# Eighty unread 384-column products behind the rounded exponentials of the first ten units

## The chip, the core and the metric

The program runs on one core of a Trainium2 chip. A core has a matrix engine (TensorE, PE in the profile, with its weight loads shown as PEld), VectorE (DVE), ScalarE (ACT), GpSimd (POOL), SyncE (SP, which here only issues transfers) and 16 DMA engines. Each engine works through its own list of instructions in order and waits on semaphores of the others. The metric is the device time of one execution in microseconds (us); a comparison takes the median of several runs.

## The reference

Biased attention is followed by a two-layer network with a sigmoid gate. Shapes: 4 batches, 8 heads, 576 positions, head size 64; 2304 tokens of width 512, hidden width 2048.

```python
scores = q @ k.T / 8
x = log1p(|i - j|) / log1p(max(i, 1))
bias = relu(x * w1 + b1) @ w2              # 32 hidden values, one result per head
attn = softmax(scores + bias); out = attn @ v
x = out as [2304, 512]
h = x @ w_in; g = h * sigmoid(1.702 * h); result = g @ w_out
```

Everything comes and goes as 4-byte floats, the weights as 8-byte floats that the kernel takes apart as 32-bit words.

## The kernel before

**Precision.** Each large product is made of three products of 16-bit halves: an operand is scaled, rounded to 16 bits (the high part), and the rest is kept as a second 16-bit tile (the low part, made by `lo_part`, L218, or at L382, L420, L508).

**Units.** The attention is cut into 72 units: two heads of one batch for one chunk of 128 query rows (a chunk has 64 rows at the end). The first 36 units are for batches 0 and 1. For unit u the written program does, in this order:

- `emit_s`: 12 products into the score tile `sp` (L349). The pool `ps_s` has one such tile, so the scores of the next unit wait until this one is read.
- `emit_soft1`: per head VectorE adds the bias tile `bt` and finds the maximum (L365, called *the maximum* here), ScalarE takes the exponential (L369), VectorE makes the reciprocal of the sum (L376, L377), ScalarE or VectorE writes the rounded exponentials into `hl` (L381 or L379, called *the rounding*), VectorE writes their low part (L382). Then one DMA transposes `hl` into `aT` (L391, issued by SP).
- `emit_av`, two to four units later: 30 products of `aT` with the values (L414) into a tile `ot`, which VectorE reads out to `xT` (L419, L420).
- steps of the network on token blocks that are finished: `emit_m1` (12 products into `hp`, L492, then L498, L500, L505 or L507, L508) and `emit_m2` (products into `op`, L522).
- a share of splitting the weights (`split_w`): three bit operations (L456, L459, L462), a rounding (L468) and a low part (L218) for each of 32 pieces: one piece after each of the units 0 to 7, four after each of the units 8 to 13.
- a share of the bias tables (`bias_hidden`, four activations L163 or L165; `bias_products`, 16 products L183 and L185; the copy L189; the store L190), up to unit 28.
- loads and transposes for later units, among them `trans_k_own` (L285, L292, with read-outs L287, L294 and L218), which makes the keys `kT` of heads 4 to 7: of batch 0 after unit 2 (needed by unit 4), of batch 1 after unit 4 (needed by unit 6).

**Banks.** The pool `ps_h` has two banks, which are given out in turn, in the written order, to `pc`, `kt`, `kp`, some `qp`, every `ot` and every `hp`. Whoever gets a bank waits until its last user has been read or, where nobody reads it, written.

**Order.** The order on each engine isn't the written one: a scheduler goes through the program with its own estimate of time and lets an instruction go ahead as soon as its operands and banks are free by that estimate. One instruction more can so move others far away.

Of the kernel before, what the change touches and what calls it, by code (L numbers as in the profile page):

```python
# [7 lines left out]
F32 = mybir.dt.float32  # L8
# [12 lines left out]
def kernel(  # L21
# [26 lines left out]
    nc = tc.nc  # L48
# [41 lines left out]
    ps_h = ctx.enter_context(tc.tile_pool(name="ps_h", bufs=2, space=PSUM))  # L90
# [120 lines left out]
    def stage(shape, dt, tag, name):  # L211
        return wk.tile(shape, dt, tag=tag, name=name, bufs=BUFS[tag])
# [143 lines left out]
    def emit_soft1(u):  # L356
        bt = bt_t[u]
        at = wk.tile([128, 2 * S], F32, tag="a32", name="a32", bufs=BUFS["a32"])
        mx = wk.tile([128, 2], F32, tag="mx", name="mx")
        sm = wk.tile([128, 2], F32, tag="sm", name="sm", bufs=6)  # L360
        hl = wk.tile([128, 2, 2 * S], F16, tag="hl", name="hl", bufs=BUFS["hl"])
        for a in range(2):
            cs = slice(S * a, S * a + S)

            nc.vector.tensor_tensor_reduce(  # L365
                out=at[:, cs], in0=s_ps.pop((u, a))[:, 0:S], in1=bt[:, cs], scale=-1.0 / BS, scalar=3.0e38,
                op0=ALU.add, op1=ALU.min, accum_out=mx[:, a:a + 1],
            )
            nc.scalar.activation(  # L369
                out=at[:, cs], in_=at[:, cs], func=ACTF.Exp, scale=-1.0, bias=mx[:, a:a + 1],  # L370
                accum_out=sm[:, a:a + 1],
            )
        for a in range(2):
            cs = slice(S * a, S * a + S)
            r = sm[:, a:a + 1]
            nc.vector.tensor_scalar(out=r, in0=r, scalar1=1.0e-9, scalar2=1.0 / AS, op0=ALU.add, op1=ALU.mult)  # L376
            nc.vector.reciprocal(out=r, in_=r)  # L377
            if a < VEC_EXP.get(u, 0):
                nc.vector.tensor_scalar(out=hl[:, 0, cs], in0=at[:, cs], scalar1=r, scalar2=None, op0=ALU.mult)  # L379
            else:  # L380
                nc.scalar.activation(out=hl[:, 0, cs], in_=at[:, cs], func=ACTF.Identity, scale=r)  # L381
            nc.vector.scalar_tensor_tensor(  # L382
                out=hl[:, 1, cs], in0=at[:, cs], scalar=r, in1=hl[:, 0, cs], op0=ALU.mult, op1=ALU.subtract
            )

        if u in AT_W:
            x = 8 * 2 * DM + 18 * 128 * AT_W[u]
            t = wo16.rearrange("p f x d -> p (f x d)")[:, x:x + 18 * 128].rearrange("p (c n) -> p c n", c=18)
        else:
            t = stage([128, 18, 128], F16, "aT" if u <= max(BIAS_A) or u % 4 < 2 else "ht", "aT")  # L390
        nc.sync.dma_start_transpose(out=t, in_=hl.rearrange("p x n -> p (x n)"))  # L391
        aT[u] = t
# [262 lines left out]
    for u in range(NU + 2):  # L655
        if u < NU:
            emit_s(u)
            emit_soft1(u)
        ready = NF * sum(1 for x in last_unit if x < av)
        late = u - AV_LAG.get(u, 2) in last_unit[1:]  # L660
        if not late:
            msteps(ready, STEPS_A.get(u, 1))
        while av <= u - AV_LAG.get(u, 2):
            emit_av(av)
            av += 1
        if late:
            msteps(ready, STEPS_A.get(u, 1))
        elif u - 2 == last_unit[0]:
            ready = NF
        if u < len(W_STEPS):  # L670
            weights_to(w_done[1] + W_STEPS[u])
        if u in BIAS_A:
            bias_first()
        msteps(ready, STEPS_B.get(u, 1))
        bias_second()
        if u in BIAS_B:
            bias_first()
            bias_second()
        if u + BIAS_AHEAD < NU:
            bias_get(u + BIAS_AHEAD)  # L680
        for fn, args in todo.get(u, ()):
            fn(*args)
# [56 lines left out]
```

## Time and profile before

| | us |
|---|---|
| median of 3 runs | 725.68 (724.52 to 728.96) |
| the profiled execution | 725.27 |
| its span, first to last instruction | 723.5 |
| TensorE busy | 642.0 (89%) |
| VectorE busy | 514.7 (71%) |
| ScalarE busy | 408.1 (56%) |
| mean granted clock of TensorE | 0.959 of full |

A busy share is a mean over the whole span. The kernel has a front part, in which the bias tables, the splitting of the weights and the first units go on together, and a long rest, in which TensorE is nearly always busy, so the engines have to be read by stretches. The granted clock has two levels, 1.2 and 2.4 GHz; a mean of 0.75 means half of the time at either.

### The profile page before, as it was taken

The numbers are of one execution on the slowest core, as the hardware profiler recorded it, in microseconds if no ns is written. First come the engines' busy times: TensorE is split into PE (matmuls) and PEld (weight loads), VectorE is DVE, ScalarE is ACT, GpSimd is POOL, SyncE is SP. The second block draws the span as 40 slices with busy tenths as digits, with TensorE's granted clock in tenths as the row PEclk, the third lists the DMA queues.
The fourth block names the chain that finished last, engine by engine and source line by source line (L and its number), as shares of the span: only waits on it lengthen the run. The fifth ranks groups of instructions, "written<-read, shape, count | busy, mean of one in ns | idle before, by whom it ended". The sixth has DMA issues, their size and how long they took to land. (4 is left out here: it accounts for less than half of the span.)

```text
span 723.5 us, 17516 instructions
## 1 busy us (share of the span) xinstructions
PE 642.0 (89%) x6888; PEld 385.0 (53%) x6888; DVE 514.7 (71%) x1416; ACT 408.1 (56%) x847; POOL 133.9 (19%) x194
## 2 busy tenths in 40 slices
PE   5655777869969999999979899899999999999997
PEld 3212333425536655656646465566666666666765
DVE  6865998798957766777677877855775896775321
ACT  6897978686558655665544446743443453343133
POOL 1202000111201111212221112121222222212222
PEclk9967978998989999999999999999999999999999
DMA  9889999968997656867576789955564475745000
GB/s 241 236 259 237 240 241 289 259 158 221 216 175 174 132 116 134 178 149 154 127 173 115 164 146 148 189 134 107 100 129 106 100 167 126 122 77 96 2 31 15
DMA packets 230771, 111.80 MB, mean 155 GB/s; under 512 B 210720, under 2 KB 214944, under 8 KB 230688
## 3 DMA queue, kind: packets, MB, share of 16 engines
q1 hardware_dynamic: 222592, 94.65, 62.7%
q10 hardware_dynamic: 7952, 15.43, 7.0%
q8 instruction: 54, 0.88, 0.5%
q0 software_dynamic: 144, 0.59, 0.2%
q14 instruction: 29, 0.24, 0.1%
HBM read 52.85 MB, written 15.34 MB: 94 GB/s over the span
## 5 line engine op out<-in xcount | busy, mean ns | idle before, releaser
L492 PE MATMUL hp<-xT,wi 128*128 128x256 f16 (+1 forms) x1920 | 216.9, 265 | 4.5 <-DVE th L500 3.6
L522 PE MATMUL op<-wo,gT 128*128 128x512 f16 x864 | 214.4, 381 | 4.9 <-DVE sm L376 2.4
L508 POOL TENSOR_TENSOR gT<-th,gT 128x256 f16<-128x256 f32 (+1 forms) x160 | 118.5, 742 | 513.0 <-DVE gT L507 279.9
L492 PEld LDWEIGHTS <-wi 128*128 128x128 f16 x1920 | 168.0, 98 | 48.5 <-issue 15.7
L369 ACT ACTIVATE a<-a,mx 128x576 f32<-128x576 f32 x144 | 110.4, 767 | 107.2 <-DVE mx L365 104.5
L382 DVE SCALAR_TENSOR_TENSOR hl<-a,sm,hl 128x576 f16<-128x576 f32 x144 | 121.7, 854 | 16.9 <-ACT hl L381 16.6
L365 DVE CUSTOM_DVE_ANT_0 a<-sp,bt 128x576 f32<-128x576 f32 x144 | 103.0, 752 | 35.5 <-PE sp L349 30.5
L522 PEld LDWEIGHTS <-gT 128*128 128x128 f16 x864 | 78.9, 98 | 84.1 <-POOL gT L508 5.1
L498 ACT ACTIVATE th<-hp 128x256 f32<-128x256 f32 (+1 forms) x160 | 56.4, 353 | 114.6 <-PE hp L492 109.6
L500 DVE SCALAR_TENSOR_TENSOR th<-th,hp 128x256 f32<-128x256 f32 (+1 forms) x160 | 62.2, 390 | 76.2 <-ACT th L498 76.0
L414 PE MATMUL ot<-aT,v 128*64 128x128 f16 (+1 forms) x2280 | 79.5, 221 | 26.8 <-DMA aT<-hl 25.2
L414 PEld LDWEIGHTS <-v 128*64 128x64 f16 x2400 | 69.5, 114 | 63.2 <-issue 43.1
L381 ACT ACTIVATE hl<-a,sm 128x576 f16<-128x576 f32 x103 | 76.3, 766 | 30.0 <-DVE sm L377 11.9
L183 PE MATMUL o<-ht,pk 128*32 128x512 f32 x288 | 69.6, 690 | 17.2 <-ACT os L189 13.8
L163 ACT ACTIVATE ht<-tab,pk 128x576 f32<-128x576 f32 x96 | 78.3, 860 | 9.3 <-PE o L185 5.0
L349 PE MATMUL sp<-kT,qT 64*128 64x512 f16 (+2 forms) x960 | 72.1, 292 | 8.2 <-DVE mx L365 5.9
L349 PEld LDWEIGHTS <-qT 64*128 64x128 f16 (+1 forms) x960 | 29.6, 98 | 56.9 <-issue 26.9
L419 DVE TENSOR_SCALAR xT<-ot 128x128 f16<-128x128 f32 x72 | 20.4, 284 | 22.1 <-PE ot L414 21.8
L507 DVE CAST gT<-th 128x256 f16<-128x256 f32 x112 | 32.6, 291 | 3.5
L376 DVE TENSOR_SCALAR sm<-sm 128x1 f32<-128x1 f32 x144 | 21.0, 149 | 16.2 <-ACT a L369 15.5
L189 ACT ACTIVATE os<-o,oc 128x576 f32<-128x576 f32 x36 | 26.3, 730 | 10.2 <-PE o L185 9.4
L165 DVE TENSOR_SCALAR ht<-tab,pk,b1n 128x576 f32<-128x576 f32 x48 | 26.9, 609 | 4.9 <-PE o L185 4.9
(57 smaller groups left out, 416.3 us busy)
## 6 DMA issues: line engine op xcount, KB each, us to landing
bt<-scr SPq DMA_DIRECT2D x31, 576.0 KB, 4.6
scr<-os ACTq DMA_DIRECT2D x36, 288.0 KB, 5.0
w<-in_moe_w_in_dram SPq DMA_DIRECT2D x16, 512.0 KB, 5.1
w<-in_moe_w_out_dram SPq DMA_DIRECT2D x16, 512.0 KB, 5.6
k<-in_k_dram SPq DMA_DIRECT2D x32, 128.0 KB, 3.9
q<-in_q_dram SPq DMA_DIRECT2D x16, 256.0 KB, 4.6
out_dram<-ob ACTq DMA_DIRECT2D x16, 256.0 KB, 3.0
bt<-scr SPq DMA_DIRECT2D x8, 288.0 KB, 4.1
```

Source lines behind the costliest of these rows:

```text
L163: nc.scalar.activation(out=h, in_=tv, func=ACTF.Relu, bias=b1c, scale=sc[:, col:col + 1])
L183: nc.tensor.matmul(om[po], lhsT=w2b, rhs=h[:, :, 0:128], start=True, stop=True)
L349: nc.tensor.matmul(ps[a][64 * e:64 * e + m, cs], lhsT=qt[r, x, hp + e, 0:m], rhs=kT[b, hp + e][r, y, cs], start=i == 0, stop=i == 2,)
L365: nc.vector.tensor_tensor_reduce(out=at[:, cs], in0=s_ps.pop((u, a))[:, 0:S], in1=bt[:, cs], scale=-1.0 / BS, scalar=3.0e38, op0=ALU.add, ...
L369: nc.scalar.activation(out=at[:, cs], in_=at[:, cs], func=ACTF.Exp, scale=-1.0, bias=mx[:, a:a + 1], accum_out=sm[:, a:a + 1],)
L381: nc.scalar.activation(out=hl[:, 0, cs], in_=at[:, cs], func=ACTF.Identity, scale=r)
L382: nc.vector.scalar_tensor_tensor(out=hl[:, 1, cs], in0=at[:, cs], scalar=r, in1=hl[:, 0, cs], op0=ALU.mult, op1=ALU.subtract)
L414: nc.tensor.matmul(o[64 * a:64 * a + 64, po], lhsT=vt[:, x, vc:vc + 64], rhs=t[:, 9 * y + k0, po], start=kb < 0 and i == 0, stop=kb == 3 a ...
L492: nc.tensor.matmul(p[:, :n], lhsT=wi16[:, x, cc, 128 * f:128 * f + 128], rhs=r, start=i == 0, stop=i == 11,)
L500: nc.vector.scalar_tensor_tensor(out=g[:, :n], in0=th[:, :n], scalar=1.0, in1=p[:, :n], op0=ALU.add, op1=ALU.mult)
L508: nc.gpsimd.tensor_tensor(out=gt[:, 1, :n], in0=g[:, :n], in1=gt[:, 0, :n], op=ALU.subtract)
L522: nc.tensor.matmul(op_t[j, i], lhsT=gt[:, x, ts], rhs=wo16[:, f, y, :], start=f == 0 and n3 == 0, stop=f == NF - 1 and n3 == 2,)
```

## The change

In `emit_soft1`, for the units 0 to 9, a tile `wm` of `ps_h` is taken for each head after its rounding, and four products of 128 by 384 columns, with a weight load each, multiply the high part with itself into that tile. Nobody reads it. That is 10 x 2 x 4 = 80 products on TensorE and 20 more turns of the two banks.

```diff
             else:
                 nc.scalar.activation(out=hl[:, 0, cs], in_=at[:, cs], func=ACTF.Identity, scale=r)
+            if u < 10:
+                e = hl[:, 0, cs]
+                w = ps_h.tile([128, 512], F32, tag='h', name='wm')
+                for _ in range(4):
+                    nc.tensor.matmul(w[:, 0:384], lhsT=e[:, 0:128], rhs=e[:, 128:512], start=True, stop=True)
             nc.vector.scalar_tensor_tensor(
                 out=hl[:, 1, cs], in0=at[:, cs], scalar=r, in1=hl[:, 0, cs], op0=ALU.mult, op1=ALU.subtract
             )
```

No other instruction is added or dropped on any engine; the others are put in another order. The numbers behind the names are those of the tiles and differ between the two programs; from L386 on the changed program's lines stand five higher. From unit 17's scores and exponentials on the order is that of before, apart from a few neighbours on TensorE up to the twentieth tile `hp`.

TensorE, keys of heads 4 to 7 of batch 0. Before, their transposes (`kt_595`, and `kp_601`, `kp_608`) stand among the first bias products, and the scores of unit 4 (`sp_699`) come behind the first value products (`ot_730`):

```order
L285 MATMUL kt_595<-idn_74,kt32_94 128x64 x2
L273 MATMUL kp_175<-idn_74,k32_87 128x128 x4
...
L185 MATMUL o_489<-ht_486,pk_76 32x64 x2
...
L414 MATMUL ot_730<-aT_371,v16_327 64x128
L285 MATMUL kt_782<-idn_74,kt32_101 128x64 x2
...
L349 MATMUL sp_699<-kT_596,qT_230 128x512
```

Now the same transposes (`kt_625`, `kp_631`, `kp_638`) come behind the added products of unit 2, and unit 4's scores (`sp_739`) behind them:

```order
L386 MATMUL wm_572<-hl_555 128x384
L285 MATMUL kt_625<-idn_74,kt32_94 128x64 x2
L292 MATMUL kp_631<-idn_74,k32_134 128x128 x4
L183 MATMUL o_611<-ht_605,pk_76 32x512 x2
...
L292 MATMUL kp_638<-idn_74,k32_134 128x128 x4
...
L349 MATMUL sp_739<-kT_626,qT_230 128x512
```

The transposes moved from ahead of unit 0 to behind unit 2's rounding, and the first value products to behind unit 5's scores.

ScalarE, between the exponentials of unit 5 (`a32_817`, now `a32_867`) and of unit 6 (`a32_915`, now `a32_975`). Before:

```order
L369 ACTIVATE a32_817,sm_819<-a32_817,mx_818 128x576 x2
L190 DMA scr1_80<-os_590 128x576
L248 ACTIVATE qT_899<-qp_894 128x512
L468 ACTIVATE wo16_73<-w32_1071 128x512
L468 ACTIVATE wi16_72<-w32_1202 128x512
L369 ACTIVATE a32_915,sm_917<-a32_915,mx_916 128x576 x2
```

Now:

```order
L369 ACTIVATE a32_867,sm_869<-a32_867,mx_868 128x576 x2
L473 ACTIVATE wi16_72<-w32_1292 128x512
L163 ACTIVATE ht_936<-tab_75,pk_76 128x576 x2
L189 ACTIVATE os_728<-o_719,oc_78 128x576
...
L287 ACTIVATE kT_833<-kt_832 128x2x64
...
L294 ACTIVATE kT_833<-kp_838 128x512
...
L189 ACTIVATE os_1059<-o_1050,oc_78 128x576
...
L473 ACTIVATE wi16_72<-w32_1308 128x512
L369 ACTIVATE a32_975,sm_977<-a32_975,mx_976 128x576 x2
```

Twelve activations of bias tables, three copies, three roundings of weights and the three read-outs of the keys of batch 1 now lie between the two exponentials, where two roundings and one read-out lay.

SP, the load of the seventh piece of weights (`w64_763`, now `w64_813`) and the transposes of the units 0 and 1 (`aT_371` and `aT_455`, now `aT_381` and `aT_475`). Before:

```order
L391 DMA_TRANSPOSE aT_371<-hl_358 128x18x128
L204 DMA bt_593<-scr0_79 128x1152
L311 DMA v32_693<-in_v_dram 64x2x256
L315 DMA v32_693<-in_v_dram 64x2x64
L437 DMA w64_763<-in_moe_w_out_dram 128x1024
L391 DMA_TRANSPOSE aT_455<-hl_442 128x18x128
L204 DMA bt_691<-scr0_79 128x1152
```

Now:

```order
L396 DMA_TRANSPOSE aT_381<-hl_358 128x18x128
L204 DMA bt_623<-scr0_79 128x1152
L396 DMA_TRANSPOSE aT_475<-hl_452 128x18x128
L204 DMA bt_731<-scr0_79 128x1152
L307 DMA v32_733<-in_v_dram 64x2x256
L311 DMA v32_733<-in_v_dram 64x2x256
L315 DMA v32_733<-in_v_dram 64x2x64
L442 DMA w64_813<-in_moe_w_out_dram 128x1024
```

The piece of weights moved behind the transposes of unit 1, the second bias load and three loads of values.

## Rows read from the trace of the kernel before

**Rows 1.** Head of the page.

```profile
span 723.5 us, 17516 instructions
```

**Rows 2.** Busy time by stretches, cut at the maxima of units 6, 10, 17.

```profile
core 0: us, PE busy (x) PEld busy (x) DVE busy (x) ACT busy (x) POOL busy (x), PEclk, DMA share, GB/s
30.00:86.66 56.66, 35.31 (x300) 14.55 (x296) 42.21 (x105) 48.92 (x87) 5.46 (x6) 0.79 1.01 250
86.66:143.31 56.65, 44.15 (x418) 19.46 (x418) 49.14 (x120) 45.33 (x76) 3.27 (x3) 0.88 1.03 266
143.31:219.48 76.17, 59.38 (x595) 33.12 (x590) 63.77 (x163) 49.02 (x91) 11.17 (x11) 0.91 0.86 189
219.48:723.50 504.02, 484.11 (x5413) 307.98 (x5411) 339.51 (x991) 242.09 (x561) 106.47 (x154) 0.99 0.60 122
```

**Rows 3.** Timeline, value products and their readers: start, duration, [idle before, releaser].

```profile
63.04 1.81 PE L414 MATMUL ot<-aT,v 128*64 128x128 f16 x30 [5.22 <-DMA aT<-hl]
64.89 0.29 DVE L419 TENSOR_SCALAR xT<-ot 128x128 f16<-128x128 f32 x1 [4.53 <-PE ot L414]
...
211.62 1.81 PE L414 MATMUL ot<-aT,v 128*64 128x128 f16 x30 [5.63 <-DMA aT<-hl]
...
213.47 0.29 DVE L419 TENSOR_SCALAR xT<-ot 128x128 f16<-128x128 f32 x1 [5.58 <-PE ot L414]
```

**Rows 4.** Timeline of TensorE, twelve 256-column products at either clock.

```profile
213.37 2.74 PE L492 MATMUL hp<-xT,wi 128*128 128x256 f16 x12
...
219.66 1.48 PE L492 MATMUL hp<-xT,wi 128*128 128x256 f16 x12
```

**Rows 5.** Timeline of VectorE, the first maxima of units 4, 6, 10 and 17.

```profile
74.15 0.75 DVE L365 CUSTOM_DVE_ANT_0 a<-sp,bt 128x576 f32<-128x576 f32 x1
...
86.66 0.74 DVE L365 CUSTOM_DVE_ANT_0 a<-sp,bt 128x576 f32<-128x576 f32 x1
...
143.31 0.75 DVE L365 CUSTOM_DVE_ANT_0 a<-sp,bt 128x576 f32<-128x576 f32 x1
...
219.48 0.76 DVE L365 CUSTOM_DVE_ANT_0 a<-sp,bt 128x576 f32<-128x576 f32 x1
```

**Rows 6.** Timeline and DMA issues, the seventh piece of weights and its neighbours.

```profile
59.29 0.60 SPq L315 DMA_DIRECT2D v<-in_v_dram  x1
59.93 0.60 SPq L437 DMA_DIRECT2D w<-in_moe_w_out_dram  x1
60.63 5.91 SPq L391 DMA_TRANSPOSE aT<-hl  x1
...
71.56 0.41 DVE L456 TENSOR_SCALAR w<-w 128x512 uint32<-128x512 uint32 x1
...
w<-in_moe_w_out_dram SPq DMA_DIRECT2D x16, 512.0 KB, 5.6
```

**Rows 7.** Groups of ScalarE: busy us in all, mean ns of one.

```profile
L369 ACT ACTIVATE a<-a,mx 128x576 f32<-128x576 f32 x144 | 110.4, 767 | 107.2 <-DVE mx L365 104.5 <-issue 2.5
L163 ACT ACTIVATE ht<-tab,pk 128x576 f32<-128x576 f32 x96 | 78.3, 860 | 9.3 <-PE o L185 5.0 <-DVE pk L134 2.8 <-ACT ht L163 0.7
L189 ACT ACTIVATE os<-o,oc 128x576 f32<-128x576 f32 x36 | 26.3, 730 | 10.2 <-PE o L185 9.4 <-DMA out_dram<-ob 0.5
L468 ACT ACTIVATE wi<-w 128x512 f16<-128x512 f32 x16 | 9.7, 620 | 1.8 <-DVE w L462 1.8
```

**Rows 8.** Groups of VectorE, the kinds of work that moved.

```profile
L382 DVE SCALAR_TENSOR_TENSOR hl<-a,sm,hl 128x576 f16<-128x576 f32 x144 | 121.7, 854 | 16.9 <-ACT hl L381 16.6
L500 DVE SCALAR_TENSOR_TENSOR th<-th,hp 128x256 f32<-128x256 f32 (+1 forms) x160 | 62.2, 390 | 76.2 <-ACT th L498 76.0
L459 DVE SCALAR_TENSOR_TENSOR w<-w,w 128x512 uint32<-128x512 uint32 x32 | 22.5, 702 | 0.0
L419 DVE TENSOR_SCALAR xT<-ot 128x128 f16<-128x128 f32 x72 | 20.4, 284 | 22.1 <-PE ot L414 21.8
L218 DVE SCALAR_TENSOR_TENSOR wi<-w,wi 128x512 f16<-128x512 f32 x16 | 10.9, 684 | 3.7 <-ACT wi L468 3.7
```

## The prediction

> **What bounds the kernel now.** I cut the span of 723.5 us [rows 1] where unit 6, unit 10 and unit 17 reach VectorE with their first maximum, at 86.66, 143.31 and 219.48 us [rows 5], and read the busy times of each stretch [rows 2]. Behind 219.48 TensorE is busy 484.11 of 504.02 us at a clock of 0.99: there it is the bound. Ahead of it no engine is. From 30 us to unit 6 ScalarE leads (48.92 of 56.66 us busy); from unit 6 to 10 and from 10 to 17 VectorE does (49.14 of 56.65, 63.77 of 76.17), and TensorE stands idle for 21.4, 12.5 and 16.8 us, at clocks of 0.79, 0.88 and 0.91. The transfers are close to full as well (DMA share 1.01, 1.03, 0.86). So one question decides: when does unit 17 arrive? From there the order of all engines is as before, and a shift of unit 17 moves the end by as much, since TensorE has only 19.9 us of idle time in which to give it back.
>
> **The products themselves.** Twelve products of 256 columns took 1.48 us at the upper level and 2.74 at the lower [rows 4], so 0.123 and 0.228 each; by columns one of 384 takes 0.185 or 0.343, and 80 of them 14.8 or 27.4 us. 72 stand ahead of unit 10's scores: 13.3 to 24.7 us. In their place 90 value products, four groups `hp` and 12 products `op` left that stretch for the one behind. An `hp` group is 1.48 us; 30 value products took 1.81 at the lower level [rows 3], some 1.0 at the upper as an estimate by the ratio of rows 4; 12 products of 512 columns are some 2.9 by columns. Together 3.0 + 5.9 + 2.9 = 11.8 us. Up to unit 10 TensorE's work therefore grows by 2 to 13 us against the 33.9 idle there: hidden. Between unit 10 and 17 its 59.38 us grow by those 11.8 and the last 8 added products (1.5), less a remainder that is still to come, to some 72 of 76 us. That is the price that can show.
>
> **What waits newly, unit 4.** Each tile `wm` takes one of two banks, so the transposes of the keys for unit 4 can't start before unit 2's rounding. On SP the seventh piece of weights now goes behind unit 1's transposes, a bias load and three loads of values. Those transposes occupied SP from 60.63 for 5.91 us [rows 6]; with some 0.6 each for the four loads the piece is issued at 69 instead of 59.93, and lands 5.6 later at 74.6, while VectorE took it up at 71.56 before. Behind it on VectorE, ahead of unit 4's maximum, stand the rest of that splitting (3 x 0.70), two low parts of `hl` (2 x 0.85), some three low parts (3 x 0.68) and two bit operations (1.4) [rows 8]: 7 us. Unit 4 comes at 81 instead of 74.15.
>
> **Unit 6.** Its scores stand behind the keys of batch 1, those behind bias products, and these wait for ScalarE, which now has between the exponentials of unit 4 and unit 6: 16 bias activations (78.3 / 96 = 0.816 each), 4 copies (0.73), 4 roundings of weights (0.61), 4 exponentials (0.77), 2 roundings (0.77) and 3 read-outs (0.6 at most) [rows 7]: 13.1 + 2.9 + 2.4 + 3.1 + 1.5 + 1.5 = 24.5 us. Starting at 82, it arrives at 106; unit 6's maximum may lie up to 3 ahead of that: 103, against 86.66. VectorE stands still for part of that time, but it also gets work done early: two pieces of weights are split ahead of unit 6 more than before, and both heads of unit 5 are finished: six bit operations (4.2 at most), three low parts of weights (2.1), two roundings and two low parts (3.4 at most), less one read-out (0.6): 9 us.
>
> **Unit 10.** From unit 6 to 10 VectorE had 49.14 us. Off go the 9 just named, and what moved behind unit 10: one piece of weights with its low parts (2.1 + 1.4), six operations on `xT` (1.7), two low parts (1.7), seven on `th` and `gT` (2.7 at most) [rows 8], 9.5 in all, leaving 30.6. ScalarE's share shrinks by the 16 activations and 4 copies to under 30, so VectorE leads. It idled for 7.5 us here before; with 5, unit 10 comes at 103 + 30.6 + 5 = 138.6 instead of 143.31. The late unit has caught up, because the bias and weight work that overtook it is then done.
>
> **Unit 17.** VectorE has 63.77 + 9.5 = 73.3 us up to it and idled for 12.4 before. Of these, 5.58 lay ahead of one read-out at 213.47, which waited on value products that waited 5.63 for their transposes [rows 3], with the next scores queued behind on TensorE. In the new order two groups `hp`, 12 products `op` and bias products stand between the scores of unit 16 and those value products, so part of that wait is covered. I take 8 us of idle time: 138.6 + 73.3 + 8 = 219.9, or 0.4 later than 219.48. With 725.27 for the profiled execution that is 725.7, **726 us**; the median of 725.68 is 0.4 above the execution I add to.
>
> The bounds: with 3 us idle from unit 6 to 10 and 3 from 10 to 17, unit 17 comes at 213, or 719 us. With the 7.5 and 12.4 of before it comes at 227, and if the splitting that is late at unit 4 costs its whole 5.91 again in a longer landing, at 233: 739.
>
> **Rival one: faster.** Value products now stand behind later scores, so the two places where they held up everything behind them, 4.53 and 5.58 us of idle VectorE [rows 3], may both go, and 725.3 - 10.1 = 715. For it: the wait at 63.04 goes surely, as the first value products now follow unit 5's scores. Against it: what comes next there is ScalarE, which is 86% busy. The granted clock works in the same direction: 0.79 and 0.88 ahead of unit 10 mean that TensorE was at the lower level for 42% and 24% of the time, 37 us of which it was busy in some two thirds; at the upper level all along that work would take 12 us less. But TensorE idles 33.9 us there, and its speed only counts where VectorE or ScalarE waits for it. The Trainium skill ("TensorE: Matmul & The Clock Gate", "Why this matters for your kernels") advises to keep TensorE busy and to leave no gaps between bursts, since gaps bring the lower clock; by that rule alone this filling would pay the 12 us, about 714. The trace bears out the clock, low just where TensorE had gaps, and not that this stretch is bound by it. Chance of this case, by either way: 0.25.
>
> **Rival two: slower.** VectorE's idle time ahead of unit 6 is never made up. From 81 to 103 it has its work of before from unit 4 to 6 (12.5 us between the maxima) and the 9 that moved, so idles little; but if unit 6 is later than 103, because each scores group waits for an added product, and this for a rounding on ScalarE, nothing else is queued on VectorE. If besides the stretches behind keep their idle time of 7.5 and 12.4, with TensorE now at 72 of 76 us, unit 17 comes at 105 + 30.6 + 7.5 + 73.3 + 12.4 = 229, or 735 us. It decides from an idle time of some 20 us on VectorE between the maxima of unit 6 and 17: as much as before is enough. The low clock at 213.37 [rows 4] shows that TensorE falls behind there when it has waited. Chance 0.28, in which lies also that the added products, all four in front of scores at the lower level, cost 1.4 us in each of some eight units (11 us, 736).
>
> **How the numbers follow.** 0.47 for 726, 0.25 for 715, 0.28 for 735. About 1% (7.3 us) is what a measurement of this kernel can tell from no change: the three cases give faster 0.25, same 0.47, slower 0.28. The range takes in the bounds 719 and 739 and most of rival one: 714 to 740.
>
> **What would show it.** In the changed trace: unit 4's maximum at 79 to 83 behind a wait of VectorE for a weight load; unit 6's at 100 to 107 with ScalarE full ahead of it; unit 10's at 137 to 145; unit 17's within 7 us of 219.48; TensorE busy for some 72 us from unit 10 to 17; and from there to the end 504 us as before. If that last stretch differs by more than 3 us, the argument that only unit 17 counts is wrong. If unit 6 is in time, the count of ScalarE's work was no bound; if the clock from 30 to 143 us stays where it was, the products don't fill the gaps at all.

## The result, and the profile after

The changed kernel took 720.63 us (median of 9 runs, 718.96 to 722.39), the kernel before 727.18 beside it (9 runs, 724.52 to 732.24): a ratio of 0.9909, 95% interval 0.9883 to 0.9935. The forecast was 726 and no change that could be measured; the time fell by 6.6 us. (Runs of the kernel before spread over 1.5% and more, and the ratios leave out what lies over 1.5% above a kernel's fastest run; so a ratio can stand nearer to 1 than the medians beside it.)

The profiled execution, 720.63 us with a span of 718.9, in the windows of [rows 2], cut at the maxima of the same units:

```profile
30.00:102.12 72.12, 52.22 (x344) 19.50 (x345) 51.88 (x117) 63.61 (x108) 5.87 (x6) 0.86 0.94 249
102.12:136.73 34.61, 23.91 (x279) 11.96 (x278) 33.78 (x88) 26.21 (x47) 0.00 (x0) 0.83 0.91 227
136.73:212.89 76.16, 67.57 (x759) 39.93 (x761) 71.35 (x182) 54.72 (x101) 14.04 (x14) 0.96 1.03 232
212.89:718.90 506.01, 486.39 (x5429) 309.91 (x5427) 340.52 (x991) 241.60 (x560) 107.39 (x154) 0.99 0.61 121
```

Unit 6 is 15.5 us later than before, unit 10 is 6.6 earlier, unit 17 is 6.6 earlier, and from there it takes 506.0 us where it took 504.0. The gain is made ahead of unit 17, and VectorE shows how: up to unit 17 it is busy 157.0 us (51.88 + 33.78 + 71.35) of 182.9, before 155.1 of 189.5 [rows 2]. So it does 1.9 more and idles 25.9 us in place of 34.4.

Where it idles less is read by stretches. Up to unit 10 VectorE has 85.66 us of work (51.88 + 33.78) where it had 91.35 (42.21 + 49.14), and idles 21.1 in place of 22.0: that brings unit 10 forward by 6.6. What was put off comes behind unit 10, where it is busy for 7.6 us more (71.35 against 63.77), and yet that stretch is as long as before (76.16 against 76.17 us): the work fills time in which VectorE had stood idle, 12.4 us before and 4.8 now. So the lead of unit 10 is not given back. The maxima, and two places that answer to [rows 3] and [rows 6], from the timelines of VectorE and SyncE of the changed kernel:

```profile
70.73 0.43 DVE L461 TENSOR_SCALAR w<-w 128x512 uint32<-128x512 uint32 x1 [5.53 <-DMA w<-in_moe_w_out_dram]
...
78.63 0.75 DVE L365 CUSTOM_DVE_ANT_0 a<-sp,bt 128x576 f32<-128x576 f32 x1
...
212.89 0.76 DVE L365 CUSTOM_DVE_ANT_0 a<-sp,bt 128x576 f32<-128x576 f32 x1
...
64.44 0.61 SPq L315 DMA_DIRECT2D v<-in_v_dram  x1
65.15 0.54 SPq L442 DMA_DIRECT2D w<-in_moe_w_out_dram  x1
```

What VectorE waited for from 30 us to unit 17, first rows of the table of waits (engine and line, what it waited for, us in total, times, longest), before:

```profile
DVE xT L419 <- PE ot L414: 13.4, 6, 5.6
DVE wo L218 <- ACT wo L468: 4.6, 3, 3.2
DVE a L365 <- DMA bt<-scr: 4.4, 2, 3.9
DVE wi L218 <- ACT wi L468: 3.7, 2, 3.6
...
DVE hl L382 <- ACT hl L381: 0.4, 1, 0.4
```

and after:

```profile
DVE wi L218 <- ACT wi L473: 7.6, 2, 5.5
DVE w L461 <- DMA w<-in_moe_w_out_dram: 6.5, 3, 5.5
DVE hl L387 <- ACT hl L381: 3.7, 5, 1.6
DVE th L505 <- ACT th L503: 2.6, 1, 2.6
DVE a L365 <- DMA bt<-scr: 2.0, 1, 2.0
```

The 13.4 us for value products (`xT` reads `ot`) are gone, all six waits. In their place stand the weight load that the prediction foresaw (6.5 us), waits for ScalarE's rounded exponentials (`hl`, 3.7 where they had been 0.4) and one for `th` (2.6). The waits for roundings of weights stayed at some 8 us (`wo` and `wi`).

Why unit 14's value products no longer wait is seen on SyncE and TensorE. Before, they waited at 211.62 [rows 3] for transposes that SyncE had issued at 200.91, 10.7 us earlier, and the scores of unit 16 stood right ahead of them:

```profile
200.91 4.99 SPq L391 DMA_TRANSPOSE aT<-hl  x1
...
205.09 0.91 PE L349 MATMUL sp<-kT,qT 64*128 64x512 f16 x12
```

After:

```profile
193.95 4.61 SPq L396 DMA_TRANSPOSE aT<-hl  x1
...
204.56 3.32 SPq L396 DMA_TRANSPOSE aT<-hl  x1
...
199.10 0.91 PE L349 MATMUL sp<-kT,qT 64*128 64x512 f16 x12
...
200.82 1.47 PE L497 MATMUL hp<-xT,wi 128*128 128x256 f16 x12
...
204.08 1.47 PE L497 MATMUL hp<-xT,wi 128*128 128x256 f16 x12
...
206.71 1.03 PE L419 MATMUL ot<-aT,v 128*64 128x128 f16 x30
...
211.46 0.55 PE L419 MATMUL ot<-aT,v 128*64 128x128 f16 x13 [0.15 <-DMA aT<-hl]
211.94 0.91 PE L349 MATMUL sp<-kT,qT 64*128 64x512 f16 x12
```

Unit 14's transposes are issued at 193.95 and its 30 value products start 12.8 us later without waiting; unit 15's are issued at 204.56, and its products wait 0.15. Counted from unit 10's maximum, the transposes of unit 14 leave at much the same time as before, 57.2 us behind it in place of 57.6. What moved is TensorE: it is ready for the value products 70.0 us behind unit 10 (at 206.71) in place of 62.7 (at 205.99, 5.63 ahead of 211.62), since other products now take it 6.7 us between the scores of unit 16 and them, a wait of 0.5 included.

The added products themselves, all 80, in the view by tile (durations ns least, median, most; what TensorE idled for ahead of them):

```profile
L386 PE MATMUL wm<-hl x80: 322/326/528, 48.2 to 142.6; 128*128 128x384 f16 x80
its engine sat idle before it (us, times) until:
  ACT hl L381: 6.9, 3
```

### The profile page after: what moved, and what is told of

The parts are those of the page before. It is cut to its first block, busy times and chain, and to the rows that moved or that the text cites. A ratio compares the mean times of both kernels' runs of the same rounds, so it can differ in the third digit from the quotient of the medians.

```text
span 718.9 us, 17683 instructions
## 1 busy us (share of the span) xinstructions
PE 647.9 (90%) x6968; PEld 390.1 (54%) x6968; DVE 516.6 (72%) x1416; ACT 408.3 (57%) x847; POOL 135.4 (19%) x194
## 4 chain that ended last, share of the span: by engine, by line
PE 55%; DVE 18%; DMA 11%; ACT 8%; issue 5%; SPq 2%; POOL 0%; ACTq 0%; DVEq 0%; POOLq 0%
PE hp L497 21%; PE op L527 19%; PE ot L419 7%; DMA aT<-hl 6%; PE sp L349 5%; DVE hl L387 3%; DVE a L365 3%; DMA v<-in_v_dram 2%; ACT ht L163 2%; DVE w L464 2%; PE o L183 2%; DVE w L467 2%; ACT a L369 2%; ACT hl L381 2%; DMA w<-in_moe_w_out_dram 1%
## 5 line engine op out<-in xcount | busy, mean ns | idle before, releaser
L419 PEld LDWEIGHTS <-v 128*64 128x64 f16 x2400 | 66.9, 112 | 33.7 <-issue 27.3
L419 PE MATMUL ot<-aT,v 128*64 128x128 f16 (+1 forms) x2280 | 75.7, 217 | 9.3 <-DMA aT<-hl 6.4
L183 PE MATMUL o<-ht,pk 128*32 128x512 f32 x288 | 60.9, 686 | 19.5 <-ACT os L189 16.1
L183 PEld LDWEIGHTS o<-ht,pk 128*32 128x32 f32 x288 | 10.0, 114 | 40.5 <-ACT os L189 19.8
L376 DVE TENSOR_SCALAR sm<-sm 128x1 f32<-128x1 f32 x144 | 21.3, 149 | 14.5 <-ACT a L369 13.6
```

Source lines behind the costliest of these rows:

```text
L183: nc.tensor.matmul(om[po], lhsT=w2b, rhs=h[:, :, 0:128], start=True, stop=True)
L419: nc.tensor.matmul(o[64 * a:64 * a + 64, po], lhsT=vt[:, x, vc:vc + 64], rhs=t[:, 9 * y + k0, po], start=kb < 0 and i == 0, stop=kb == 3 a ...
```

## Experiments

The change does three things at once: it adds work, it adds waits and bank turns, and it makes the scheduler arrange the whole program anew. By the orders of the two kernels 359 of TensorE's 6596 products, 208 of VectorE's 1272 instructions, 99 of ScalarE's 759 and 26 of SyncE's 240 stand at another place. **Theory A**: the gain is the order's. **Theory B**: the products pay, by keeping TensorE's clock up. **Theory C**: the order pays and the products cost.

To hold an order, `_in_order` runs once the program is written and chains every instruction of an engine to the one that is to stand ahead of it, without a semaphore (the filling products of fill_before and order_fill are left out of the chain, and the scheduler places them):

```python
        for d in struct.unpack("<%dh" % (len(raw) // 2), raw):
            at += d
            i = traced[e][at]
            if prev is not None:
                tc.add_manual_dep(i, prev.name, info, reason="order")
            prev = i
```

All runs in one table (us; unit 17 is its first maximum in the profiled execution, the rest is that execution's span behind it; groups of rows by chip, each with its own runs of the kernel before, whose median is the last column):

| run | median | ratio (95%) | unit 17 | rest | before |
|---|---|---|---|---|---|
| order_alone | 721.29 | 0.9960 (0.9926 to 0.9995) | 209.11 | 509.8 | 726.52 |
| order_tiny | 719.69 | 0.9931 (0.9899 to 0.9963) | 213.81 | 506.5 | 726.52 |
| fill_before | 724.42 | 0.9995 (0.9962 to 1.0028) | 218.29 | 506.6 | 726.52 |
| before_sp14 | 731.12 | 1.0088 (1.0056 to 1.0120) | 222.39 | 507.6 | 726.52 |
| hl14_early | 725.42 | 1.0002 (0.9968 to 1.0036) | 216.38 | 506.4 | 726.26 |
| order_w6 | 720.31 | 0.9914 (0.9880 to 0.9948) | 210.72 | 510.4 | 726.26 |
| order_eight | 723.25 | 0.9942 (0.9909 to 0.9975) | 212.28 | 507.7 | 726.26 |
| tiny_free | 738.10 | 1.0159 (1.0110 to 1.0209) | 226.38 | 513.2 | 726.26 |
| hl14_bias | 722.87 | 0.9962 (0.9940 to 0.9984) | 213.87 | 506.8 | 725.37 |
| order_late14 | 728.91 | 1.0051 (1.0024 to 1.0077) | 217.01 | 514.1 | 725.37 |
| one_free | 744.42 | 1.0250 (1.0210 to 1.0289) | 230.16 | 514.1 | 725.37 |
| eight_free | 733.57 | 1.0097 (1.0059 to 1.0136) | 230.83 | 502.8 | 725.37 |
| after_again | 720.03 | 0.9937 (0.9914 to 0.9960) | 211.63 | 505.4 | 725.31 |
| order_alone_again | 722.42 | 0.9959 (0.9931 to 0.9987) | 210.36 | 507.0 | 725.31 |
| order_fill | 723.56 | 0.9991 (0.9965 to 1.0017) | 216.63 | 508.8 | 725.31 |

**order_alone**: the kernel before, no added product, in the changed kernel's order.

```diff
         tile_bias_attention__then__act_sigmoid_gelu_kernel(tc, *args)
+        _in_order(nc, tc)
```

> The kernel before, none of the added products, with every engine's instructions put by hand in the order that they have in the changed kernel. Theory A (the gain comes from the order in which the changed program is scheduled, not from the products): 718 to 722 us, VectorE takes the maximum of unit 17 near 213 as in the changed kernel (212.89), and the wait of 5.6 us for unit 14's transposes is gone. Theory B (the products keep TensorE's clock up and that pays): no products, no gain, 725 to 729, with the granted clock from 30 us to unit 17 back from about .92 to about .89. Theory C (the products cost a little and the order pays more): 715 to 719, since ScalarE's 6.9 us of idle behind the products is gone too.

It is faster than before, by 5.2 us of median (the ratio makes it 2.9). Unit 17 comes at 209.11, 10.4 ahead of before and 3.8 ahead of the changed kernel, so the order alone makes all the gain there is up to unit 17. The rest took 509.8, and so the end is where the changed kernel's is. Its windows, and two windows of 5 us from the rest:

```profile
30.00:99.20 69.20, 45.21 (x325) 16.88 (x322) 50.48 (x117) 62.99 (x107) 6.22 (x6) 0.80 0.96 254
99.20:134.30 35.10, 19.05 (x221) 9.74 (x220) 33.85 (x88) 26.18 (x47) 0.00 (x0) 0.72 0.89 228
134.30:209.11 74.81, 65.82 (x752) 39.72 (x754) 71.25 (x183) 54.52 (x101) 14.03 (x14) 0.97 0.98 233
...
460.00:465.00 5.00, 1.73 (x17) 1.55 (x17) 2.19 (x6) 3.78 (x10) 0.00 (x0) 0.79 0.90 232
465.00:470.00 5.00, 5.00 (x22) 2.59 (x21) 3.37 (x8) 2.54 (x7) 2.17 (x4) 0.53 0.14 31
```

From unit 6 to 10 the clock is 0.72, less than the 0.88 of before [rows 2], and yet unit 10 comes at 134.30. That speaks against theory B. What gave 3.8 us back behind unit 17 is told at the end.

**order_tiny**: the changed kernel in its own order with 8 columns per added product; their waits, banks and places stay.

```diff
-                    nc.tensor.matmul(w[:, 0:384], lhsT=e[:, 0:128], rhs=e[:, 128:512], start=True, stop=True)
+                    nc.tensor.matmul(w[:, 0:8], lhsT=e[:, 0:128], rhs=e[:, 128:136], start=True, stop=True)
```

> The changed kernel in its own order, each added product cut from 384 to 8 columns: their waits for the rounding, their turns in the banks and their places stay, their work is gone. Theory A: as the changed kernel, 719 to 722. Theory B (work and clock): 725 to 729. Theory C: between the changed kernel and the one with the order alone, 716 to 720, nearer to the first if the waits and turns cost, nearer to the second if the columns do.

719.69: with a 48th of the columns the gain is all there. Theory B falls by this too.

**fill_before**: the order before, and 80 products of 384 columns that wait for no rounding and no bank, in spare columns of the score tiles.

```diff
+        if u < 10:
+            f = kT[b, hp][:, 0]
+            for a in range(2):
+                for _ in range(4):
+                    nc.tensor.matmul(pair[:, a, 576:960], lhsT=f[:, 0:128], rhs=f[:, 128:512], start=True, stop=True)
```

> The kernel before in its own order, with 80 products of 384 columns in its first ten units that wait for no rounding and take no bank of their own (they write spare columns of the score tile behind the scores). Theory A: the order is that of before, so 726 to 730, the products costing nothing or a little. Theory B: granted clock of the first 143 us up from .86 to .9 or more, and 720 to 724. Theory C: as A.

```profile
30.00:87.79 57.79, 43.34 (x360) 17.62 (x356) 43.13 (x107) 48.85 (x87) 5.45 (x6) 0.91 1.02 246
87.79:144.39 56.60, 44.38 (x442) 21.00 (x442) 49.42 (x120) 45.23 (x76) 3.72 (x3) 0.97 1.06 263
144.39:218.29 73.90, 59.97 (x595) 33.20 (x590) 63.68 (x164) 49.05 (x91) 11.15 (x11) 0.91 0.83 196
```

The clock rises from 0.79 to 0.91 and from 0.88 to 0.97, and the two stretches take 57.79 and 56.60 us where they took 56.66 and 56.65 [rows 2]. Filling saves nothing there. The Trainium skill ("TensorE: Matmul & The Clock Gate", "Why this matters for your kernels") advises to keep TensorE busy and to leave no gaps between its products. The trace agrees on the clock, and of the 12 us that the prediction had worked out for a higher clock the time shows none. What the fillers cost is in this: TensorE is busy for 8.0 us more up to unit 6 (43.34 against 35.31), and two maxima of VectorE wait 2.3 us for fillers. So the run shows that filling doesn't pay, and not what a higher clock alone would be worth.

**before_sp14**: the order before, with ten loads on SyncE behind unit 14's transposes that stood ahead of them.

```diff
+L204 DMA bt<-scr_81 128x1152
+L391 DMA_TRANSPOSE aT<-hl 128x18x128
 L302 DMA v_4404<-in_v_dram 128x2x256
 L306 DMA v_4404<-in_v_dram 64x2x64
...
-L204 DMA bt<-scr_81 128x1152
-L391 DMA_TRANSPOSE aT<-hl 128x18x128
```

> The kernel before in its own order but for one thing on SyncE: ten loads for the later batches (five v, four k, one q) that stand ahead of unit 14's transposes are issued behind them. Theory A, if the late landing of those transposes (10.7 us after issue, ot#14 waits 5.63 us on TensorE) is what the changed kernel's order removes: landing in 6 to 8 us, the wait on TensorE under 2, unit 17 at 215 to 217, and 722 to 725. If the gain is VectorE's order of work instead: unit 17 near 219 and 726 to 729 however early the transposes land. Theory B: 726 to 729.

A miss, 4.6 us slower. From the timelines of SyncE and TensorE:

```profile
200.23 4.54 SPq L391 DMA_TRANSPOSE aT<-hl  x1
...
214.06 3.67 SPq L391 DMA_TRANSPOSE aT<-hl  x1
...
210.76 1.81 PE L414 MATMUL ot<-aT,v 128*64 128x128 f16 x30 [5.05 <-DMA aT<-hl]
...
219.67 1.12 PE L414 MATMUL ot<-aT,v 128*64 128x128 f16 x25 [2.44 <-DMA aT<-hl]
```

Unit 14's transposes are issued 0.7 us earlier only, since they wait for its low parts, which VectorE wrote late, and land as late as before. SyncE stood still, first for a bias load ahead of them (issued at 199.13) and then for them, with the ten loads behind it; these then hold up unit 15's transposes, 214.06 in place of 207.25, and its value products wait 2.44 as well. So the loads were no cause, and the place of the low parts on VectorE comes into view: **theory D**, that the order gains where a unit's low parts stand further ahead of the value products that read them.

**hl14_early** and **hl14_bias** try it in the order before: unit 14's second reciprocal, its roundings (ScalarE) and its low parts (VectorE) go ahead of other work, its transposes ahead of some loads. VectorE in both:

```diff
-L377 RECIPROCAL sm<-sm 128x1
+L377 RECIPROCAL sm<-sm 128x1 x2
...
+L382 SCALAR_TENSOR_TENSOR hl<-a_2095,sm,hl 128x576 x2
...
-L377 RECIPROCAL sm<-sm 128x1
-L382 SCALAR_TENSOR_TENSOR hl<-a_2095,sm,hl 128x576
...
-L382 SCALAR_TENSOR_TENSOR hl<-a_2095,sm,hl 128x576
```

> The kernel before in its own order but for unit 14: its second reciprocal, both roundings on ScalarE and both low parts on VectorE stand right behind its first reciprocal, ahead of the bias steps and the weight splitting that stood between, and on SyncE its transposes stand ahead of the last two k pairs and a q load. Theory D (the gain of the changed order from unit 10 to 17 is that a unit's low parts, and so its transposes, stand further ahead of the value products that read them): transposes issued near 197 in place of 200.9, the 5.6 us wait of VectorE for unit 14's value products down to 1 or 2, unit 17 at 214 to 216, 720 to 724 us. Rival E (the wait only moves on: the splitting that was pushed back, or unit 15's transposes, is late in its place): unit 17 at 218 to 221 and 725 to 729.

725.42, not told from before. SyncE issued the transposes at 199.14, because a bias load ahead of them waited for a bias output that the same edit had put behind the roundings on ScalarE. VectorE's wait shrank to 3.15 us where 1 to 2 were expected, and unit 17 came at 216.38 where 214 to 216 were. hl14_bias mends it on ScalarE, and puts the bias load behind the transposes:

```diff
 L189 ACTIVATE os<-o,oc 128x576
-L163 ACTIVATE ht<-tab,pk 128x576 x2
-L381 ACTIVATE hl<-a_2095,sm 128x576
-L190 DMA scr_82<-os 128x576
+L190 DMA scr_82<-os 128x576
+L381 ACTIVATE hl<-a_2095,sm 128x576 x2
+L163 ACTIVATE ht<-tab,pk 128x576 x2
```

> hl14_early again with its fault mended: there unit 14's transposes stood behind a bias load on SyncE that waited for ScalarE's bias output, which the edit itself had made late. Here the bias output goes first on ScalarE and the bias load stands behind the transposes. Theory D (distance between a unit's low parts and its value products): transposes issued at 196 to 198 in place of 199.1 (200.9 before), VectorE's wait for unit 14's value products 0 to 2 in place of 3.15 (5.58 before), unit 17 at 213.5 to 215.5, 721 to 724 us. Rival E (the wait moves on): unit 17 at 217 to 220, 725 to 728.

```profile
195.72 2.84 SPq L391 DMA_TRANSPOSE aT<-hl  x1
...
204.39 1.03 PE L414 MATMUL ot<-aT,v 128*64 128x128 f16 x30
```

The transposes leave at 195.72 and the value products start at 204.39 without a wait. From unit 10 to 17 it takes 72.95 us (140.92 to 213.87) in place of 76.17, and the kernel is faster than before: 0.9962, 0.9940 to 0.9984. Of the 5.6 us by which unit 17 is earlier, 2.4 were there at unit 10, ahead of the edit: so much two executions differ. The stretch from unit 10 to 17 by itself proves little: hl14_early took 72.23 us for it and fill_before, with no edit there, 73.90. That early low parts pay rests on the ratio of hl14_bias; it overlaps with that of hl14_early, so how much they pay is open.

**order_late14** is the mirror of it: the changed kernel's order, no products, with unit 14's low parts late.

```diff
-L382 SCALAR_TENSOR_TENSOR hl<-a_2095,sm,hl 128x576
 L456 TENSOR_SCALAR w_2025<-w_2011 128x512
-L382 SCALAR_TENSOR_TENSOR hl<-a_2095,sm,hl 128x576
...
+L382 SCALAR_TENSOR_TENSOR hl<-a_2095,sm,hl 128x576 x2
 L382 SCALAR_TENSOR_TENSOR hl<-a_2229,sm,hl 128x576 x2
```

> The mirror of it: the changed kernel's order without the products, in which unit 14's two low parts stand on VectorE behind some 7 us of other work, ahead of unit 15's low parts, as they stand late in the order before. Theory D: transposes issued near 198 in place of 190, the value products of unit 14 wait 2 to 6 us on TensorE where they waited for none, unit 17 at 212 to 215 in place of 209.1, 723 to 726 us. Rival E (the place of one unit's low parts is worth nothing): unit 17 within 1 of 209.1 and 720 to 722.

728.91, 6.5 over order_alone_again on the same chip (7.6 over order_alone): two instructions that stand later on VectorE, so that the transposes leave at 198.44 and not at 190.34, undo the whole gain. The place was not where I had expected it:

```profile
198.44 2.72 SPq L391 DMA_TRANSPOSE aT<-hl  x1
...
207.98 4.19 SPq L391 DMA_TRANSPOSE aT<-hl  x1
...
204.62 1.03 PE L414 MATMUL ot<-aT,v 128*64 128x128 f16 x30
...
214.51 0.91 PE L414 MATMUL ot<-aT,v 128*64 128x128 f16 x13 [5.29 <-DMA aT<-hl]
```

Unit 14's value products still find their transposes (198.44 to 204.62). But SyncE waited for them until 198.44, with loads behind, and unit 15's transposes leave at 207.98 in place of order_alone's 200.62. Unit 15's value products wait 5.29, the scores of unit 17 stand right behind them, and unit 17 comes at 217.01. As in before_sp14, the price of a late unit goes by SyncE's queue to the next one.

**order_w6**: order_alone, with the seventh weight piece ahead of unit 1's transposes again.

```diff
+L437 DMA w_763<-in_moe_w_out_dram 128x1024
 L391 DMA_TRANSPOSE aT<-hl 128x18x128
...
-L437 DMA w_763<-in_moe_w_out_dram 128x1024
```

> The kernel with the changed kernel's order and no added products, one SyncE entry moved back: the seventh weight piece is loaded ahead of unit 1's transposes and not behind them and three v loads. As the prediction had it (that wait costs VectorE 5 us before unit 4 and nothing behind unit 6, since ScalarE leads there): unit 4 at 72 to 74 in place of 76.6, unit 6 within 1 of 99.2, the end within 1 of order_alone's 721.3. Rival: the wait is on the path, unit 6 at 95 to 96, unit 17 at 205 to 206, and 716 to 718. Third: the piece's buffer is not yet free at that place, unit 1's transposes wait behind it and the end is 1 to 4 us later.

```profile
74.04 0.77 DVE L218 SCALAR_TENSOR_TENSOR wo<-w,wo 128x512 f16<-128x512 f32 x1 [3.77 <-ACT wo L468]
```

VectorE's 5.0 us for the load are gone, and 3.8 for ScalarE stand in their place; unit 4 comes at 76.76 (order_alone 76.57) and not earlier as expected, unit 6 at 100.75 (99.20), the end at 720.31, within 1 of order_alone's. ScalarE leads there, as the prediction had it.

**order_eight**: the changed kernel's order with eight products per group.

```diff
-            for _ in range(4):
+            for _ in range(8):
```

> The changed kernel in its own order with eight products in place of four in each of the twenty groups, so twice the added columns. If the products are free beside the work of other engines: as with four, 719 to 722. If they cost what TensorE's busy time in the changed kernel suggests (80 products of 0.33 us and the 6.9 us of waits for the rounding, of which order_alone shows 3.8 us gained up to unit 17): another 3 to 5 us up to unit 17, which goes to 216 to 218, and 722 to 726. If their work pays through the clock: granted clock over .93 in all stages up to unit 10, and under 719.

723.25, and unit 17 at 212.28, as with four. Twice the work costs nothing that shows up to unit 17; the medians leave room for 2 to 3 us in all.

**tiny_free, one_free and eight_free**: the changed kernel with 8 columns, one product or eight products, the order left to the scheduler. The first has the diff of order_tiny, the others these:

```diff
-            for _ in range(4):
+            for _ in range(1):
```

```diff
-            for _ in range(4):
+            for _ in range(8):
```

> The changed kernel with each added product cut from 384 to 8 columns, and the order left to the scheduler, which puts it otherwise than either kernel (some 320 rows of difference on VectorE against the changed kernel). If a changed order is as likely to lose as to gain: anywhere from 715 to 735, and its time follows VectorE's idle time up to unit 17 (before 34 us, changed order 24 to 27), with 504 to 508 us behind unit 17. If the changed kernel's gain comes from the products' turns in the banks or their waits rather than from one lucky order: 718 to 722, as with the order held.

> The changed kernel with one added product of 384 columns in place of four in each group, the order left to the scheduler. If the time is the order's and any change of it throws the dice again: 715 to 740, apart from both kernels, VectorE's waits up to unit 17 telling which way. If fewer products are simply a smaller part of the same effect: 722 to 725, between the two kernels.

> The changed kernel with eight added products of 384 columns in place of four in each group, the order left to the scheduler. If the time is the order's: 715 to 740, apart from both. If the effect grows with the products' work: with the gain, 714 to 718; with their cost, 722 to 727 as in order_eight (723.3).

738, 744 and 734, all slower than before, by 1.0 to 2.5%. The same text with 8 columns takes 719.69 us in the changed kernel's order and 738.10 in the one that the scheduler gives it. Nothing grows or shrinks with the products' work: each length throws the dice anew, and of four throws only the changed kernel's was a gain. In one_free unit 4 is at 88.89 behind two weight loads, of which VectorE's longest waits are

```profile
DVE w L461 <- DMA w<-in_moe_w_in_dram: 8.8, 3, 6.6
DVE w L461 <- DMA w<-in_moe_w_out_dram: 5.5, 1, 5.5
```

**after_again, order_alone_again and order_fill**, on one chip: do the products add to the order's gain? The first two are as before; the third is order_alone with the products of fill_before.

> The changed kernel itself, for comparison on the same chip with the two that follow. 719 to 722 us, as before.

> The kernel with the changed kernel's order and none of the added products, on the same chip as the changed kernel. If the order gives all of the gain: within 2 us of after_again, at a ratio to the kernel before whose interval overlaps that of after_again. If the products add to it through the clock: 3 us or more above after_again. If they only cost: 2 to 4 below it, as the first maximum of unit 17 at 209.1 against 212.9 would have it.

> The changed kernel's order, with 80 products of 384 columns in the first ten units that wait for no rounding and take no bank (spare columns of the score tiles) in place of the change's own products. If the clock up to unit 10 matters in this order: granted clock over .9 there in place of about .78, unit 17 two or more us ahead of order_alone's 209.1, and 716 to 719. If it doesn't, since TensorE is not what the first units wait for: unit 17 at 208 to 212 and 719 to 722.

720.03 and 722.42, with intervals that overlap (0.9914 to 0.9960, 0.9931 to 0.9987): the order gives most of the gain or all of it. Some 2 us are not told apart, though order_tiny, with the products' waits and banks but hardly any of their work, lay 1.6 below order_alone in the same direction. order_fill has the clock at 0.90 up to unit 6, and five maxima of VectorE wait 5.1 us for its fillers. Its profiled execution, the slowest of its 12 at 727.19, reaches unit 17 at 216.63, 6.3 later than order_alone_again. By the median of 723.56 it is 3.5 slower than after_again, and not told apart from order_alone_again. Filling doesn't pay here either; that it costs is likely and not shown by the medians.

What wasn't tried is the changed kernel's products in the order before: the banks that they share are handed out in the order of the program text, and that order doesn't go with it.

## Why the prediction was wrong

**Unit 4** at 81 behind a wait for the weight piece: 78.63, behind a wait of 5.53. Right in its mechanism; SyncE issued the piece at 65.15 and not at 69, since unit 1's transposes left at 57.94 and not at 60.63. That the wait costs nothing behind unit 6 was right (order_w6).

**Unit 6** at 103: 102.12. Right, by ScalarE's share (63.61 of 72.12 us busy).

**Unit 10** at 138.6, from 30.6 us of work and 5 of idling: 136.73, from 33.78 and 0.83. 3.2 us more work, 4.2 less idling, and 0.9 from unit 6. That the late unit catches up was right.

**Unit 17 is the step that failed, by its idle time**: 73.3 us of VectorE's work and "8 us of idle time". The work measured 71.35, the idle time 4.81. Together with unit 10 that is 136.73 + 71.35 + 4.81 = 212.89 in place of 219.9. Of these 7.0 us 3.2 are idle time, 1.9 work, and 1.9 were there at unit 10. Behind unit 6 the sum had 5 + 8 = 13 us of idle time, and 0.83 + 4.81 = 5.64 came. That is the prediction's own lower bound, 3 and 3 us, with unit 17 at 213 and 719 us.

The mechanism was the one given there, and its size was off. The prediction took it that two groups `hp`, 12 products `op` and bias products between the scores of unit 16 and the value products of unit 14 cover only "part of that wait" of 5.58 us [rows 3]. They keep TensorE for 6.7 us (200.0 to 206.71), and the whole wait is gone. That alone takes the idle time from 12.4 to 6.8 us; the other 2.0 are smaller waits, which no run takes apart.

The other end of the wait, when the transposes leave, can do the same. In the old order, where nothing covers the wait, hl14_bias has the low parts earlier, removes it and is faster by 0.2 to 0.6% (its interval). In the new order order_late14 puts the two low parts back and loses 6.5 us, but at unit 15, whose transposes come late by SyncE's queue; the prediction had no term for that queue. That the earlier units gained by a cover as well was not tried one by one: all six waits went, 13.4 us, and 8.5 us less idle time remained, since waits for the weight load and for ScalarE came in their place. With 1.9 us more work that is the 6.6 at unit 17.

**Rival one**, at a chance of 0.25, had the direction right: the time fell. Both of its waits for value products went, as it said; 715 was too low, since it took off 10.1 us and left out the waits that took their place and the added work. The 720.63 measured lies as far from 715 as from 726. Its other way, the clock, is not the cause: order_alone has the gain at a lower clock from unit 6 to 10, order_tiny has it without the work, and fill_before and order_fill raise the clock and gain nothing.

**Rival two** did not come about: from unit 6 to 17 VectorE idled 5.6 us, and it needed 20.

**The products' work** of 14.8 to 27.4 us was 13.6 by difference: up to unit 17 TensorE is busy 143.7 us, in order_alone 130.1, where the other products ran at a lower clock (0.86, here 0.90). Hidden, as said, though from unit 10 to 17 TensorE was busy for 67.57 us and not for some 72. The waits for the rounding, 6.9 us in three, are on TensorE. Unit 17 is 1.3 to 3.8 us later with the products (after_again against order_alone_again, and the first pair); two executions of one order lie 1.3 apart (209.11, 210.36), so a price is likely and its size open.

**The rest** at 504 us was 506.0 and 505.4, within the 3 us that I had allowed. But the argument that a shift of unit 17 moves the end by as much doesn't hold that closely: with the same order from unit 17 on, the rest was 509.8 and 510.4 in order_alone and order_w6 and 514.1 in order_late14.

## What to carry to other kernels

Where a scheduler sets the order, an edit that adds an instruction is first of all another order of the whole program; hold the order before asking what the instruction itself costs, and don't expect the next such edit to go the same way. A wait that ends a chain is judged by both its ends: what the waiting engine has to do until then, and when the other engine's late step lets the transfer leave, with all that stands behind that transfer in its queue. Where the runs to be compared differ by some us early on, times are counted from a common event, here unit 10's maximum, before it is said which end moved. A clock that is low where an engine has nothing to do need not be a loss: raising it by filling gained nothing here, where other engines were waited for.

## What the runs showed of the hardware

Behind unit 17 TensorE is the bound, and there a wait can cost more than itself. In order_alone TensorE waits 3.27 us ahead of 463.82 and runs the 5 us from 465, busy all through, at 0.53 of the clock (the two windows above): by estimate (5 us x 0.47) some 2.4 us of work less than at the full clock. In the changed kernel the same stretch, at the same place in the order, has two waits of half that length, and the clock stays up (timeline of TensorE, then the two windows):

```profile
462.34 1.51 PE L497 MATMUL hp<-xT,wi 128*128 128x128 f16 x24 [1.42 <-DVE xT L425]
...
466.61 2.14 PE L497 MATMUL hp<-xT,wi 128*128 128x128 f16 x24 [1.45 <-DVE th L505]
```

```profile
460.00:465.00 5.00, 3.56 (x44) 2.41 (x44) 4.12 (x14) 3.88 (x10) 0.43 (x1) 1.00 1.09 249
465.00:470.00 5.00, 3.55 (x35) 2.36 (x34) 3.65 (x11) 4.66 (x14) 0.81 (x2) 1.00 0.91 220
```

Counted in windows of 5 us behind unit 17 with the clock below 0.85 (adjoining ones are one fall, the last 5 us of a run are left out), order_alone and order_w6 have four such falls, and the rest took 509.8 and 510.4 us; order_late14 has five and took 514.1. The seven traces with three falls took 506.4 to 508.8, the three with two (before, the changed kernel, order_tiny) 504.0 to 506.5, and after_again with one 505.4. The falls and the length of the rest go together; why an arrival at unit 17 brings the waits together or apart was not tested.
